# Three of seven butterflies of a spectral layer made by extra stage-3 matmuls instead of by VectorE

## The chip, the cores and the metric

The kernel runs on one core of one Trainium2 chip. The metric is device time in microseconds (us) of one execution; below it is the median of several runs. A profiled execution gives the trace. Its times count from the start of the recorded span, which is some 1.8 us shorter than the device time (181.9 us for 183.7).

The engines are TensorE (PE in the profile, its weight loads PEld), VectorE (DVE), ScalarE (ACT), GpSimd (POOL) and the DMA queues. In the traces read here TensorE, VectorE and ScalarE take up their instructions in program order; e5 below shows what that can cost, 0.67 us. The granted clock in some views is the share of TensorE's full clock that the profile shows.

## The reference

The layer is a layer norm, a two-dimensional real FFT over 2048 x 512, a multiplication with complex weights, the inverse FFT and a residual; then a second layer norm and a two-layer feed-forward part with a squared ReLU.

```python
x = A_x                                           # 1 x 2048 x 512, bf16
X = rfft2(layernorm(x)); X = X * (w_r + 1j*w_i)   # 2048 x 257 complex
h = x + irfft2(X)
u = relu(layernorm(h) @ w1 + b1)
out = h + (u * u) @ w2 + b2                       # inner size 1792
```

## The kernel before

The FFT along the sequence is split in two (stages 1 and 3 forward, 4 and 6 back), with the FFT along the row between them (2 and 5). The columns of stage 3 come in pairs: pr = 0 is special, and pairs 1 to 7 have a symmetry. For those, stage 3 makes only the sums A and B by four matmuls of 512 columns. ScalarE copies them from PSUM, where the matmuls leave their sums, to SBUF, the memory that VectorE reads here (AB), and VectorE forms the four results X as A plus or minus B: the butterfly, two operations of 128x512. Then VectorE multiplies X by the weights (mA, mB), combines them into Z, and forms M, the butterfly for the way back. Stage 4 on TensorE reads M.

```python
def stage2(pr):                       # cut
    U = fwd.tile([P, 2, 512], BF16, tag="U", bufs=3)
    # ... 8 matmuls of 256 columns into pu
    nc.scalar.copy(Uv, pu[:]...)

def stage3(pr):                       # pr > 0
    px = mm_tile("p3")
    nc.tensor.matmul(px[:, 0:512], lhsT=C, rhs=U[:, 0, :], start=True, stop=False)
    nc.tensor.matmul(px[:, 0:512], lhsT=Sn, rhs=U[:, 1, :], start=False, stop=True)
    nc.tensor.matmul(px[:, 512:1024], lhsT=C, rhs=U[:, 1, :], start=True, stop=False)
    nc.tensor.matmul(px[:, 512:1024], lhsT=Sp, rhs=U[:, 0, :], start=False, stop=True)
    nc.scalar.copy(AB[:]..., px[:])

def butterfly(pr):                    # cut: two VectorE operations, returned as a pair
    return (lambda: nc.vector.tensor_tensor(Xf[:, 0::3], AB[:, 0], bsw, ALU.add),
            lambda: nc.vector.tensor_tensor(Xf[:, 2:0:-1], AB[:, 0], bsw, ALU.subtract))

def spectral(pr):                     # one "round" of VectorE, cut
    nxt = butterfly(pr + 1) if pr + 1 < 8 else (lambda: None, lambda: None)
    # mA = X * w_r ; mB = X * w_i     two operations of 128x1024
    nxt[0]()
    # Z[:, :, 0] = mA - mB ; Z[:, :, 1] = mA + mB
    nxt[1]()
    # M[:, 0] = sum, M[:, 1] = difference of the halves of Z: two operations of 128x512

stage2(0); stage2(1); stage3(0); stage3(1); stage2(2)
# tables EI for pairs 1 to 3 (transposes on TensorE, copy on ScalarE)
stage3(2)
for pr in range(9):
    if 0 < pr and pr + 2 < 8:
        stage3(pr + 2)
    if pr + 3 < 8:
        stage2(pr + 3)
    if pr > 0:
        stage4(pr - 1)                # ScalarE copies its result to T2
    # pr >= 5: five matmuls that keep TensorE busy
    if pr < 8:
        spectral(pr)
    # pr == 0: EI of pairs 1, 3 negated on VectorE; tables EI for pairs 4 to 7 built
    # pr == 1: EI of pairs 4 to 7 negated on VectorE
    # pr == 4: table GI made by ScalarE (a sine)
```

"Round" below means one call of `spectral`, numbered by its pair. The order on ScalarE: it copies AB(k), then U(k+1), then the result T of stage 4.

## Time and profile before

| | before |
|---|---|
| device time, median of 3 runs | 183.8 us |
| TensorE, VectorE, ScalarE, GpSimd busy, share of the span | 88%, 67%, 56%, 26% |
| the spectral stage (26.4 to 52.1 us) | VectorE 3.22 us a round |
| the stretch after it (to 181.9 us) | 119.8 of 129.8 us busy on TensorE |

The view of busy time by stretch, for two rounds in the middle of the stage. After the two ends and the length come busy us (and number of instructions) of TensorE, its weight loads, VectorE, ScalarE and GpSimd, then the granted clock, the DMA share and GB/s:

```profile
36.30:39.50 3.20, 2.89 (x23) 2.05 (x22) 3.20 (x10) 2.96 (x4) 0.00 (x0) 1.00 0.00 0
39.50:42.80 3.30, 2.99 (x24) 2.15 (x22) 3.30 (x10) 3.06 (x5) 0.00 (x0) 1.00 0.02 5
```

VectorE is busy for the whole of both stretches.

### The profile page before, as it was taken

Reading aid. Unit: us, or ns where it says so; the run is one execution under the profiler, and the core shown is the slowest. Engines: PE = TensorE matmul, PEld = TensorE weight load, DVE = VectorE, ACT = ScalarE, POOL = GpSimd, SP = SyncE. Lnnn points to the kernel's source line nnn. Section 1 sums busy time; section 2 is a strip of 40 time slices with the busy share of each in tenths; the row PEclk is TensorE's granted clock in tenths of the full one; section 3 lists DMA queues with packets and bytes.
Section 4 is the critical chain, followed back from the end, with each engine's and each line's share of the span. In section 5 each row is a group of like instructions: output and inputs, shape, how many; then the busy total and the mean of one; then the engine's idle time right before and its main releaser. Section 6 shows DMA issues by size and latency. Waiting matters only on the chain.

```text
span 181.9 us, 2667 instructions
## 1 busy us (share of the span) xinstructions
PE 160.0 (88%) x946; PEld 89.0 (49%) x946; DVE 122.2 (67%) x297; ACT 101.8 (56%) x172; POOL 46.5 (26%) x83
## 2 busy tenths in 40 slices
PE   3676896989978787999999999999999989999991
PEld 1244564666534475456643545544544434556440
DVE  7986549999957277646897248697338795359311
ACT  4976879999634278037931367922357921268200
POOL 5889910000000250204402022422022422025000
PEclk9999999999999999999999999999999999999999
DMA  5999990000000000000000000001110000110010
GB/s 159 352 425 405 378 228 23 0 0 4 2 0 0 2 4 0 2 29 29 4 0 29 29 29 4 0 0 50 36 34 0 0 0 29 58 34 0 0 58 29
DMA packets 7773, 11.19 MB, mean 62 GB/s; under 512 B 2256, under 2 KB 6224, under 8 KB 7504
## 3 DMA queue, kind: packets, MB, share of 16 engines
q1 hardware_dynamic: 7600, 10.11, 16.3%
q0 software_dynamic: 160, 0.92, 1.2%
q8 instruction: 7, 0.11, 0.3%
q14 instruction: 6, 0.05, 0.1%
HBM read 8.93 MB, written 2.10 MB: 61 GB/s over the span
## 4 chain that ended last, share of the span: by engine, by line
PE 50%; DVE 29%; ACT 9%; POOL 6%; issue 4%; DVEq 0%; POOLq 0%; ACTq 0%
PE ph L570 22%; PE po L589 20%; DVE act L574 3%; PE p L473 3%; DVE mA L379 3%; DVE mB L379 3%; DVE hs L488 2%; ACT rl L573 2%; ACT Bt L241 2%; PE p L532 2%; DVE st L497 2%; DVE st L205 2%; DVE M L392 2%; DVE Z L384 2%; ACT junk L494 1%
## 5 line engine op out<-in xcount | busy, mean ns | idle before, releaser
L570 PE MATMUL ph<-UT,W 128*128 128x384 bf16 (+2 forms) x280 | 53.2, 336 | 0.7 <-ACT UT L536 0.5
L573 ACT ACTIVATE rl<-ph,b1f 128x384 bf16<-128x384 f32 (+2 forms) x70 | 41.2, 603 | 20.9 <-PE ph L570 19.5
L589 PE MATMUL po<-W,act 128*128 128x512 bf16 x224 | 50.8, 379 | 0.0
L574 DVE TENSOR_TENSOR act<-rl 128x384 bf16<-128x384 bf16 (+2 forms) x70 | 32.5, 477 | 17.2 <-ACT rl L573 16.9
L570 PEld LDWEIGHTS <-W 128*128 128x128 bf16 x280 | 27.4, 98 | 20.8 <-issue 1.4
L589 PEld LDWEIGHTS <-act 128*128 128x128 bf16 x224 | 21.6, 98 | 27.4 <-issue 3.1
L577 POOL TENSOR_TENSOR hb<-hs,b2b 128x512 f32<-128x512 bf16 x16 | 18.4, 1153 | 57.4 <-DVE act L574 55.4
L593 DVE TENSOR_TENSOR ot<-po,hb 128x512 bf16<-128x512 f32 x16 | 11.0, 689 | 18.1 <-PE po L589 18.1
L517 ACT ACTIVATE u<-hs,nm,rs 128x512 bf16<-128x512 bf16 x6 | 4.7, 808 | 25.2 <-DVE nm L514 25.2
L231 PE MATMUL p<-KFr,xs 128*128 128x256 bf16 x28 | 8.6, 334 | 4.7 <-DVE KFr L216 4.6
L488 DVE SCALAR_TENSOR_TENSOR hs<-p,xs 128x512 bf16<-128x512 f32 x16 | 10.8, 678 | 0.1
L473 PE MATMUL p<-GI,T 128*128 128x256 bf16 x64 | 9.4, 272 | 0.4 <-DVE T L415 0.4
L502 POOL TENSOR_TENSOR nm<-mv 128x1 f32<-128x1 f32 x5 | 1.5, 291 | 30.9 <-ACT junk L494 30.9
L246 PE MATMUL idle<-ones 128*128 128x512 bf16 x37 | 9.0, 379 | 0.0
L487 PE MATMUL p<-R,KI 128*128 128x512 bf16 x16 | 6.1, 381 | 3.2 <-DVE R L483 3.2
L233 PE MATMUL p<-KFr,xs 128*128 128x256 bf16 x28 | 8.6, 335 | 0.0
L246 PEld LDWEIGHTS <-ones 128*128 128x128 bf16 x45 | 4.7, 106 | 7.8 <-POOL ones L142 2.9
L205 DVE BATCH_NORM_STATS2 st<-xs 128x6 f32<-128x512 bf16 x13 | 8.3, 673 | 0.0
L360 ACT CAST AB<-p 128x1024 bf16<-128x1024 f32 x7 | 7.1, 1014 | 1.9 <-PE p L358 1.2
L417 ACT CAST T<-p 128x1024 bf16<-128x1024 f32 x7 | 7.2, 1025 | 1.8 <-PE p L410 1.8
L330 PE MATMUL p<-GF,Bt 128*128 128x256 bf16 x64 | 8.1, 273 | 0.0
L473 PEld LDWEIGHTS <-T 128*128 128x128 bf16 x64 | 6.2, 98 | 3.5 <-ACT T L414 0.9
(135 smaller groups left out, 220.5 us busy)
## 6 DMA issues: line engine op xcount, KB each, us to landing
W<-in_B_w_dram SPq DMA_DIRECT2D x2, 1792.0 KB, 19.7
out_dram<-ot SPq DMA_DIRECT2D x16, 128.0 KB, 1.8
xs<-in_A_x_dram SPq DMA_DIRECT2D x3, 512.0 KB, 5.9
WB<-in_A_w_r_dram SPq DMA_DIRECT2D x1, 1028.0 KB, 9.6
WB<-in_A_w_i_dram SPq DMA_DIRECT2D x1, 1028.0 KB, 12.2
xs<-in_A_x_dram SPq DMA_DIRECT2D x2, 256.0 KB, 3.4
b2b<-in_B_b_dram SPq DMA_DIRECT2D x1, 128.0 KB, 8.2
b1b<-in_B_b_dram SPq DMA_DIRECT2D x1, 3.5 KB, 22.8
```

What stands on the lines that cost most here:

```text
L205: nc.vector.bn_stats(st[:], xs[:, g, :])
L231: nc.tensor.matmul(o, lhsT=xs[:, g, P * t:P * t + P], rhs=KFr[:, g, 0:P].unsqueeze(1).to_broadcast([P, 2, P]), start=True, stop=False)
L246: nc.tensor.matmul(o, lhsT=ones[:, 0:P], rhs=ones[:], start=True, stop=True)
L379: nc.vector.tensor_tensor(m[:], X[:], w[:, pr:pr + step + 1:step, 1:Df].unsqueeze(2).to_broadcast([P, 2, 2, 256]), ALU.mult)
L473: nc.tensor.matmul(pe[:, 256 - 256 * e:512 - 256 * e], lhsT=T2[:, lt, g].rearrange("p q s -> p (q s)"), rhs=GI[:, lt, :], start=(r == 0), ...
L488: nc.vector.scalar_tensor_tensor(hs[:, g, :], py[:], WSC, xs[:, g, :], ALU.mult, ALU.add)
L570: nc.tensor.matmul(ph[:, 0:n], lhsT=W1[:, d, bass.ts(f, P)], rhs=UT[:, d, 0:n], start=(d == 0), stop=(d == ND - 1))
L573: nc.scalar.activation(rl[:, 0:n], ph[:, 0:n], ACT.Relu, bias=b1f[:, f:f + 1], scale=1.0)
L574: sq = nc.vector.tensor_tensor(act[:, f, 0:n], rl[:, 0:n], rl[:, 0:n], ALU.mult)
L577: add = nc.gpsimd.tensor_tensor(hb[:, g, :], hs[:, g, :], b2b[:], ALU.add)
L589: nc.tensor.matmul(po[:], lhsT=act[:, f, bass.ts(i, P)], rhs=W2[:, f, :], start=(f == 0), stop=(f == NF - 1))
L593: nc.vector.tensor_tensor(ot[:], po[:], hb[:, g, :], ALU.add)
```

## The change

VectorE is to be relieved. For pairs 2, 4 and 6, stage 3 makes all four results X itself: it accumulates the second half of the butterfly in PSUM with eight more matmuls of 256 columns. ScalarE then copies X instead of AB, and VectorE has no butterfly for these pairs. A negated cosine table Cn is added, and X gets a third buffer.

```diff
+    ON_PE = (2, 4, 6)
+    Cn = fwd.tile([P, len(ON_PE), P], BF16, name="Cn")
...
+    nc.vector.tensor_scalar(Cn[:], EF[:, ON_PE[0]:ON_PE[-1] + 1:ON_PE[1] - ON_PE[0], 1, :], -1.0, None, ALU.mult)
...
+        elif pr in ON_PE:
+            C, Sp, Sn, Cm = EF[:, pr, 1, :], EF[:, pr, 0, :], EF[:, pr, 2, :], Cn[:, ON_PE.index(pr), :]
+            px = mm_tile("p3")
+            for u in range(2):
+                o = px[:, 512 * u:512 * u + 512]
+                nc.tensor.matmul(o, lhsT=C, rhs=U[:, 0, :], start=True, stop=False)
+                nc.tensor.matmul(o, lhsT=Sn, rhs=U[:, 1, :], start=False, stop=False)
+                for r, (ws, wc) in enumerate(((Sp, C), (Sn, Cm)) if u == 0 else ((Sn, Cm), (Sp, C))):
+                    other = slice(256 - 256 * r, 512 - 256 * r)
+                    orr = o[:, 256 * r:256 * r + 256]
+                    nc.tensor.matmul(orr, lhsT=ws, rhs=U[:, 0, other], start=False, stop=False)
+                    nc.tensor.matmul(orr, lhsT=wc, rhs=U[:, 1, other], start=False, stop=(r == 1))
+            Xs[pr] = X = fwd.tile([P, 2, 2, 256], BF16, tag="X", bufs=3, name="X")
+            nc.scalar.copy(X[:].rearrange("p u r c -> p (u r c)"), px[:])
...
-        nxt = butterfly(pr + 1) if pr + 1 < 8 else (lambda: None, lambda: None)
+        nxt = butterfly(pr + 1) if pr + 1 < 8 and pr + 1 not in ON_PE else (lambda: None, lambda: None)
```

More of the change, by code (lines that the diff above doesn't have):

```diff
@@ L341, in stage3 @@
         if pr == 0:
-            Xs[pr] = X = fwd.tile([P, 2, 2, 256], BF16, tag="X", bufs=2, name="X")
+            Xs[pr] = X = fwd.tile([P, 2, 2, 256], BF16, tag="X", bufs=3, name="X")
             pxs = [mm_tile("p3"), mm_tile("p3b")]
@@ L351, in stage3 @@
                 cp(X[:, u].rearrange("p r c -> p (r c)"), pxs[u][:, 0:512])
+        elif pr in ON_PE:
[10 more added lines that the diff above has]
+                    nc.tensor.matmul(orr, lhsT=wc, rhs=U[:, 1, other], start=False, stop=(r == 1))
+            Xs[pr] = X = fwd.tile([P, 2, 2, 256], BF16, tag="X", bufs=3, name="X")
+            nc.scalar.copy(X[:].rearrange("p u r c -> p (u r c)"), px[:])
         else:
@@ L364, in butterfly @@
         AB = ABs[pr]
-        Xs[pr] = X = fwd.tile([P, 2, 2, 256], BF16, tag="X", bufs=2, name="X")
+        Xs[pr] = X = fwd.tile([P, 2, 2, 256], BF16, tag="X", bufs=3, name="X")
         bsw = AB[:, 1, ::-1, :]
```

## The prediction

> **What bounds the kernel now.** I read the shares of the final chain first, then that chain in order of time, then the timeline of one engine at a time between 22 and 66 us, where the changed code runs. The page says who carries the end:
>
> ```profile
> PE 50%; DVE 29%; ACT 9%; POOL 6%; issue 4%; DVEq 0%; POOLq 0%; ACTq 0%
> ```
>
> TensorE's half is the feed-forward part (from 62 us on), which the change does not touch. VectorE's share lies largely between 26 and 52 us, in the spectral stage. One of its eight rounds in the chain (columns: start us, us, what):
>
> ```profile
> 29.69 0.60 DVE mA L379
> 30.29 0.60 DVE mB L379
> 30.89 0.34 DVE X L369
> 31.23 0.33 DVE Z L384
> 31.56 0.34 DVE Z L385
> 31.90 0.33 DVE X L370
> 32.23 0.34 DVE M L392
> 32.57 0.33 DVE M L394
> ```
>
> The reader is to see eight operations without a hole: 2 x 0.60 + 6 x 0.335 = 3.22 us a round, and mA starts repeat at 36.25, 39.47, 42.69, 45.91 and 49.13 us: 3.22 apart. The two X lines are the butterfly of the next pair, 0.67 us. So the stage looks VectorE-bound. But a second loop runs at almost the same speed. TensorE (timeline, columns: start us, us, engine line operation, idle before):
>
> ```profile
> 37.66 0.38 PE L355 MATMUL p<-U,EF 128*128 128x512 bf16 x1 [0.31 <-ACT U L337]
> ...
> 38.30 0.38 PE L358 MATMUL p<-U,EF 128*128 128x512 bf16 x1
> ...
> 40.74 0.38 PE L355 MATMUL p<-U,EF 128*128 128x512 bf16 x1 [0.31 <-ACT U L337]
> ```
>
> and ScalarE:
>
> ```profile
> 38.76 1.01 ACT L360 CAST AB<-p 128x1024 bf16<-128x1024 f32 x1 [0.24 <-ACT T L417]
> 39.67 1.02 ACT L337 CAST U<-p 128x1024 bf16<-128x1024 f32 x1
> 40.58 1.03 ACT L417 CAST T<-p 128x1024 bf16<-128x1024 f32 x1
> ...
> 44.56 1.08 ACT L113 ACTIVATE GI<-fiI 128x1024 bf16<-128x1024 int16 x1
> 45.52 1.02 ACT L360 CAST AB<-p 128x1024 bf16<-128x1024 f32 x1
> ```
>
> Stage 3 of pair k runs from 37.66. Its result is copied (AB) from 38.76, 1.10 us later. ScalarE is in order, so the copy of the next U starts 0.91 us after that. Stage 3 of pair k+1 waits for that U and starts 1.07 us after it. 1.10 + 0.91 + 1.07 = 3.08 us: a closed loop of stage 3, its copy, the next U and the next stage 3. It has only 0.14 us a round less than VectorE. TensorE's idle 0.31 us lies inside the loop, waiting for ScalarE; it is no room for extra matmuls ahead of the AB copy.
>
> Last, VectorE's final round, which has no butterfly:
>
> ```profile
> 49.74 0.68 DVE L379 TENSOR_TENSOR mB<-X,WB 128x1024 bf16<-128x1024 bf16 x1
> 50.45 0.43 DVE L384 TENSOR_TENSOR Z<-mA,mB 128x512 bf16<-128x512 bf16 x1
> 50.79 0.42 DVE L385 TENSOR_TENSOR Z<-mA,mB 128x512 bf16<-128x512 bf16 x1
> 51.31 0.42 DVE L392 TENSOR_TENSOR M<-Z 128x512 bf16<-128x512 bf16 x1
> ```
>
> Without an X between them, mB to Z takes 0.71 us start to start instead of 0.60, and Z to M 0.52 instead of 0.34. The butterfly fills the time in which a result becomes visible.
>
> **What the Trainium skill says.** "TensorE: Matmul & The Clock Gate", section "Back-to-back issue gap", gives 262 cycles between isolated matmuls of 256 columns and 518 for 512, at 2.4 GHz 109 and 216 ns. The trace agrees: sixteen of 256 columns (L330) take 1.75 us, 109 ns each, and the four of stage 3 start 0.21 or 0.22 us apart. "Perfetto Trace Analysis", section "DVE / Act Engine Instruction", says the reported window runs on to the acknowledged write. The trace agrees: mB is listed with 0.68 us while an independent operation starts 0.60 us after it. I therefore count start to start. "VectorE: DVE Perf Modes", section "The DRAIN you can't avoid", says that a read after a write on the same engine needs a semaphore or an operation in between, and that in its test the semaphore cost nothing extra. The first fits the interleaving here; the second does not: 0.11 and 0.18 us are lost in the last round.
>
> **The change part by part.**
> Removed: the two X operations ahead of pairs 2, 4 and 6. On paper 3 x 0.67 = 2.01 us of VectorE, but each of those rounds (1, 3, 5) then looks like the last one and pays 0.11 + 0.18, so it saves 0.38 us, 1.1 us in all: rounds of 2.84 instead of 3.22.
> Added on VectorE: one negation Cn of 128x384. The EI negation of that size takes 0.28 us, 0.20 start to start. The order of instructions puts it behind the EF negation (20.66), where VectorE then idles 0.43 us until 21.64 us: hidden.
> Added on TensorE: stage 3 of pairs 2, 4, 6 has four matmuls of 512 and eight of 256 columns instead of four of 512: 8 x 0.109 = 0.87 us more each, 2.61 us in all. All of it comes before the copy, so it lies in the loop: 1.97 instead of 1.10 us.
> Moved: ScalarE's order is unchanged, with X copied in place of AB for these pairs (same 128x1024 shape, same 0.91). A third X buffer means that this copy waits for the multiply three pairs back, long done.
>
> Replay with these intervals, all in us (early rounds have 1.06 to 1.07 in place of 1.10, before the T copies begin). Stage 3 starts, before then after: pair 2 28.48, 28.48; pair 3 31.52, 32.40; pair 4 34.58, 35.47; pair 5 37.66, 39.40; pair 6 40.74, 42.47; pair 7 43.82, 46.40. Pair 7's copy comes in order behind U(7), T and the GI table: U(7) 45.33, T 46.24, GI 47.15, AB(7) 48.11 until 49.13 (before: 45.52 to 46.54). That is 3 x 0.87 = 2.61, less rounding, later.
> VectorE: round 1 starts at 29.61 as before and ends at 32.45, but the EI negation behind it now waits for the EI copy, which ScalarE starts behind U(3) at 32.25 and ends at 33.27. Round 2 starts at 33.5 (33.02 before), round 3 at 36.75, round 4 at 39.6. Its butterfly needs AB(5), whose copy ends 41.5, 0.7 after VectorE could use it; round 5 starts at 43.55, round 6 at 46.4. Its multiplies end at 47.6 and its butterfly waits for AB(7) until 49.15: 1.5 us idle. X, Z, Z, X, M, M take 2.0 us, so round 7 starts at 51.2 instead of 49.13: **2.05 us late**.
> Against the 2.61 us the difference is the slack there was: X(7) ran at 47.12 with AB(7) ready at 46.54.
> After round 7 all follows as before (stage 4, stage 5, then TensorE's stretch), so the 2.05 us goes through whole: 183.8 + 2.05 = 185.85.
>
> **The rivals.**
> First, VectorE stays the bound: then 1.1 us (0.4 a round) to 2.0 us are gained, 181.8 to 182.7. For it speaks the final chain, where VectorE is named without a break. Against it speaks that the other loop is only 0.14 us a round faster, so a mean of 0.44 us more per pair turns it over.
> Second, the added matmuls hide in TensorE's idle 0.3 us a round: then the loop grows by about 0.56 instead of 0.87 three times, and the time is near 184.9. Against it: that idle time is a wait for U, behind the copy that the added matmuls delay. It would need stage 3 to start earlier, which nothing in the change does.
> Third, the delay is worse: a longer last drain, an accumulation that stalls when matmuls alternate halves of a bank, or TensorE losing clock in its longer waits. Stage 3 of pair 0 already mixes 512 and 256 in one bank at 0.11 us a step, and the granted clock is 1.00 in all of this stage, so I give at most another 0.8 us.
>
> **Range and chances.** The centre is 185.8 us, 1.1% slower. Half a microsecond each way covers the waits I rounded and the 0.5 us of the EI negation; the first two rivals stretch the lower side a little: 184.8 to 186.6. Faster by over 2% would mean under 180.1, more than the removed operations hold: chance 0.01. Slower by over 2% means over 187.5, nearly twice the delay: 0.05. Within 2%: 0.94.
>
> **What would show it right or wrong.** In the profile after: stage 3 of pairs 2, 4 and 6 takes about 1.95 us to its copy; starts of stage 3 alternate near 3.95 and 3.08 us apart; VectorE waits on ScalarE's AB copy in the rounds before pairs 5 and 7, some 0.7 and 1.5 us, and on EI near 32.5 us for some 0.9 us; rounds 1, 3, 5 take 2.84 us, not 2.55; the last M starts near 53.7 instead of 51.65; and the stretch from there to the end has its old length. The chain before 52 us then names ScalarE and TensorE between the VectorE pieces. I am wrong if stage 3 of pair 3 starts before 32 us, or if VectorE has no waits in the stage. The later stretch changing length by itself would also break the sum.

## The result and the profile after

The kernel after takes 185.76 us (185.75 to 185.78, 4 runs) against 183.78 us before: the ratio is 1.0108, with a 95% interval from 1.009 to 1.0125. So it is 1.1% slower.

VectorE's busy time did fall, from 122.2 to 121.7 us of the whole, and TensorE's rose from 160.0 to 161.3. In the spectral stage alone VectorE's fell from 25.5 us (26.0 to 52.1) to 24.4 (26.0 to 54.1), 0.38 us for each of the three pairs. The shares of the final chain have moved:

```profile
PE 53%; ACT 17%; DVE 15%; POOL 6%; issue 3%; DMA 3%; SPq 0%; POOLq 0%; DVEq 0%; ACTq 0%
```

VectorE fell from 29% to 15% and ScalarE rose from 9% to 17%. The chain in order of time shows why (start us, us, what). Where it once listed one VectorE operation after another, it now reads:

```profile
37.45 0.84 ACT X L369
38.36 1.03 ACT U L340
39.43 0.38 PE p L373
...
40.49 0.89 ACT AB L378
41.42 1.02 ACT U L340
42.48 0.38 PE p L361
...
44.41 0.89 ACT X L369
```

This is the loop: copy of stage 3, copy of the next U, next stage 3. One turn with an ordinary pair (5) takes 42.48 - 39.43 = 3.05 us; the turn with pair 4 before it took 39.43 - 35.47 = 3.96 us. The timeline of TensorE shows the longer stage 3 of pair 6, its first and its last matmul:

```profile
42.48 0.38 PE L361 MATMUL p<-U,EF 128*128 128x512 bf16 x1 [0.28 <-ACT U L340]
...
44.10 0.27 PE L367 MATMUL p<-U,EF 128*128 128x256 bf16 x1
```

Its copy starts at 44.41, 1.93 us after 42.48, against 1.10 before. TensorE still idles 0.28 us ahead of the stage: the added matmuls did not use that gap. ScalarE, at the end of the loop:

```profile
47.16 1.07 ACT L115 ACTIVATE GI<-fiI 128x1024 bf16<-128x1024 int16 x1
48.12 1.01 ACT L378 CAST AB<-p 128x1024 bf16<-128x1024 f32 x1
```

AB(7) starts at 48.12 instead of 45.52. And VectorE, which had no hole between its rounds before, now waits (last column: idle time before the operation, and what ended it):

```profile
33.32 0.29 DVE L263 TENSOR_SCALAR EI<-EI 128x512 bf16<-128x512 bf16 x1 [0.92 <-ACT EI L260]
...
39.15 0.43 DVE L410 TENSOR_TENSOR M<-Z 128x512 bf16<-128x512 bf16 x1 [0.32 <-PE p L428]
...
41.53 0.43 DVE L387 TENSOR_TENSOR X<-AB 128x512 bf16<-128x512 bf16 x1 [0.41 <-ACT AB L378]
...
46.16 0.43 DVE L410 TENSOR_TENSOR M<-Z 128x512 bf16<-128x512 bf16 x1 [0.52 <-PE p L428]
...
49.16 0.43 DVE L387 TENSOR_TENSOR X<-AB 128x512 bf16<-128x512 bf16 x1 [1.03 <-ACT AB L378]
...
53.71 0.42 DVE L412 TENSOR_TENSOR M<-Z 128x512 bf16<-128x512 bf16 x1
```

In the kernel before, the last M was this:

```profile
51.65 0.42 DVE L394 TENSOR_TENSOR M<-Z 128x512 bf16<-128x512 bf16 x1
```

The last M starts at 53.71 instead of 51.65 us, 2.06 us later. From there to the end of the span it is 130.3 us in both (181.9 - 51.65, 184.0 - 53.71). So the spectral stage alone carries the difference.

### The profile page after: what moved, and what is told of

It is laid out like the page before. It is cut to its first block, busy times and chain, and to the rows that moved or that the text cites. A ratio compares the mean times of both kernels' runs of the same rounds, so it can differ in the third digit from the quotient of the medians. Undisturbed runs are those within 1.5% of the kernel's fastest.

```text
span 184.0 us, 2708 instructions
## 1 busy us (share of the span) xinstructions
PE 161.3 (88%) x970; PEld 90.8 (49%) x970; DVE 121.7 (66%) x292; ACT 101.7 (55%) x172; POOL 46.4 (25%) x83
## 4 chain that ended last, share of the span: by engine, by line
PE 53%; ACT 17%; DVE 15%; POOL 6%; issue 3%; DMA 3%; SPq 0%; POOLq 0%; DVEq 0%; ACTq 0%
PE ph L588 21%; PE po L607 20%; ACT U L340 4%; DVE act L592 3%; DMA xs<-in_A_x_dram 3%; PE p L491 3%; DVE hs L506 2%; ACT rl L591 2%; ACT AB L378 2%; ACT Bt L243 2%; PE p L550 2%; DVE st L515 2%; ACT junk L512 1%; POOL rs L523 1%; ACT X L369 1%
## 5 line engine op out<-in xcount | busy, mean ns | idle before, releaser
L592 DVE TENSOR_TENSOR act<-rl 128x384 bf16<-128x384 bf16 (+2 forms) x70 | 32.5, 478 | 17.2 <-ACT rl L591 16.9
L233 PE MATMUL p<-KFr,xs 128*128 128x256 bf16 x28 | 7.6, 305 | 5.8 <-DVE KFr L218 5.5
L554 ACT COPY UT<-p 128x768 bf16<-128x768 bf16 (+2 forms) x5 | 4.2, 842 | 6.5 <-PE p L550 6.5
L515 DVE BATCH_NORM_STATS2 st<-hs 128x6 f32<-128x512 bf16 x11 | 7.6, 689 | 0.2
```

The lines of the kernel that those rows point to most:

```text
L515: nc.vector.bn_stats(st[:], hs[:, g, :])
L592: sq = nc.vector.tensor_tensor(act[:, f, 0:n], rl[:, 0:n], rl[:, 0:n], ALU.mult)
```

## The experiments

The theory: a loop through TensorE and ScalarE (stage 3, its copy, the next U, the next stage 3) became the bound, because all added matmuls lie inside it. The main rivals: VectorE's saved work counts after all; or the added TensorE work is too much whatever the order. Ten kernels were run, all with five rounds (e1 has four runs, the others five). The kernel before, run beside them, took 183.72 us (e1 to e4), 183.71 (e5 to e8) and 183.68 (e9, e10); these three batches ran on three chips, so they agree to 0.04 us.

| run | what | us | ratio to before (95% interval) |
|---|---|---|---|
| e1 | before + the matmuls only | 185.77 | 1.0112 (1.0096 to 1.0127) |
| e2 | butterflies left out only (wrong result) | 183.12 | 0.9968 (0.9954 to 0.9982) |
| e3 | after, stage 2 ahead of stage 3 | 182.95 | 0.9959 (0.9945 to 0.9972) |
| e4 | before, stage 2 ahead of stage 3 | 183.90 | 1.0010 (0.9997 to 1.0024) |
| e5 | after, GI table late | 185.09 | 1.0074 (1.0060 to 1.0088) |
| e6 | e3, tables late, gaps filled with M | 182.39 | 0.9927 (0.9914 to 0.9941) |
| e7 | before, three X buffers | 183.79 | 1.0001 (0.9987 to 1.0015) |
| e8 | e3, tables late | 182.59 | 0.9939 (0.9925 to 0.9952) |
| e9 | e1, stage 2 ahead of stage 3 | 184.34 | 1.0035 (1.0021 to 1.0048) |
| e10 | e6, negations late, X ahead of Z | 182.24 | 0.9920 (0.9907 to 0.9934) |

### The two halves of the change, each alone

e1 adds to the kernel before as many matmuls, of the same size and at the same place, with a weight of zeros. The result stays correct and all butterflies stay on VectorE.

```diff
+    nc.gpsimd.memset(zw[:], 0.0)
...
     nc.tensor.matmul(px[:, 0:512], lhsT=Sn, rhs=U[:, 1, :], start=False, stop=not more)
+    if more:                          # pairs 2, 4, 6; the same after the second half
+        zeros(px[:, 0:512])           # four matmuls of 256 columns, lhsT=zw
```

> The kernel before with all seven butterflies on VectorE, and eight more matmuls of 256 columns with a weight of zeros in stage 3 of pairs 2, 4 and 6 (same result). Loop theory: 185.8 us like the full change, because VectorE's butterflies then run inside its waits for the pair 7 copy (ending near 49.15 us, last M start near 53.7). If the work removed from VectorE counted at all in the full change, this kernel would be slower than it by up to 1.1 to 2.0 us: 186.9 to 187.8. If the matmuls hid in TensorE's idle time: 183.8.

It took 185.77 us, as the full change did (185.76). VectorE of e1, at pair 7's butterfly and the last M:

```profile
49.26 0.43 DVE L384 TENSOR_TENSOR X<-AB 128x512 bf16<-128x512 bf16 x1 [0.37 <-ACT AB L375]
...
53.81 0.42 DVE L409 TENSOR_TENSOR M<-Z 128x512 bf16<-128x512 bf16 x1
```

With all seven butterflies VectorE still comes to pair 7 too early and waits. So in the full change the work taken from VectorE counts for nothing, and the added matmuls alone make the whole loss.

e2 is the other half: the kernel after with the four old matmuls for pairs 2, 4 and 6 and no butterfly. Its output is wrong, which doesn't matter for the time.

```diff
-            for u in range(2):
-                ...                   # twelve matmuls
+            nc.tensor.matmul(px[:, 0:512], lhsT=C, rhs=U[:, 0, :], start=True, stop=False)
+            ...                       # the four of the kernel before
```

> The kernel after without the added matmuls: the butterflies of pairs 2, 4, 6 are just left out, so the result is wrong on purpose. Loop theory: stage 3 starts stay 3.08 us apart, AB(7) ends at 46.5 us as before, VectorE comes to it about 0.6 us early and waits: 183.2 to 183.3 us, a gain of 0.5 us only. Rival, VectorE alone is the bound: 182.7 us if each butterfly is worth 0.38 us, 181.8 us if it is worth 0.67 us.

It took 183.12 us, 0.60 us less than before (its last M starts at 51.06 us against 51.65). Removing 2.0 us of VectorE operations gains only that, even when TensorE gets no more work; the loop theory had said 0.5. VectorE waits 0.41 us for AB(7), whose copy still starts at 45.46 us. Two things set that start. The loop, still at 3.05 to 3.08 us a turn, brings stage 3 of pair 7 to 43.75 us; and the GI table stands in front of the copy on ScalarE, so that it comes 1.71 us after that start and not 1.06, as in e5 below. By an estimate from these numbers, AB(7) without GI in front would be there by 45.85 us, before VectorE could use it at 46.01. So it is the loop and the GI table together, not the loop alone, that take the rest of the gain. No run has e2 with GI late.

### Opening the loop

e3 puts stage 2 of pair k+1 ahead of stage 3 of pair k. ScalarE then copies U(k+1) before the result of stage 3, and the next stage 3 no longer waits behind that copy. e4 does the same to the kernel before.

```diff
+    stage2(3)
     stage3(2)
     for pr in range(9):
+        if 0 < pr and pr + 3 < 8:
+            stage2(pr + 3)
         if 0 < pr and pr + 2 < 8:
             stage3(pr + 2)
-        if pr + 3 < 8:
-            stage2(pr + 3)
```

> The kernel after with stage 2 of pair k+1 put ahead of stage 3 of pair k, so that ScalarE copies U(k+1) before the result of stage 3 and the loop is open. Loop theory: TensorE no longer waits for U in the loop, added matmuls run in its spare time, AB(7) ends near 46.5 us and round 7 starts near 48.6 us: 183.2 us. Rival, TensorE's work itself is what bounds (added 2.61 us whatever the order): 185.8 us.

> Control: the kernel before with the same reorder. Loop theory: before the change VectorE's 3.22 us rounds bound, the loop had 0.14 us a round to spare, so opening it changes nothing: 183.8 us, at most 0.2 either way. If the loop had bound before as well: a gain of over 0.5 us.

e3 took 182.95 us: 2.8 us less than the kernel after, by order alone, with the same matmuls. AB(7) starts at 45.02 us instead of 48.12, and TensorE, which waited for U at each stage 3, has no wait listed between 28.5 and 48.3 us. The time is also 0.25 us less than expected: VectorE no longer waits for AB(7) at all. AB(7) in e3:

```profile
45.02 1.01 ACT L378 CAST AB<-p 128x1024 bf16<-128x1024 f32 x1
```

e4 took 183.90, no gain. So before the change the loop did not bind, and after it the loop did. The rival that TensorE's work itself bounds the kernel after is refuted.

e9 is e1 with this reorder, so that the matmuls alone are tried in an open loop.

> e1 (all butterflies on VectorE, added zero-weight matmuls) with the order of e3 and e4. It leaves the order as the only difference to e1. Loop theory: the same 2.61 us of matmuls now run beside VectorE: 183.9 us like e4, at most 184.2. If TensorE's work bounds whatever the order: 185.8 us like e1.

It took 184.34 us: 1.43 us less than e1, but 0.44 more than e4, where I had allowed 0.3. The trace shows where: VectorE waits 0.56 us for AB(2) in round 1 (e4 loses 0.19 there), while the pipeline is being filled and stage 3 of pair 2 is already the longer one. From round 2 on it goes at 3.22 us a round without a wait. So the matmuls are hidden once the loop is open, except for the first.

### The piece of ScalarE work inside the loop

e5 is the kernel after with the GI sine made in iteration 6 instead of 4 (a small GpSimd copy in the same branch moves with it).

```diff
-        if pr == 4:
+        if pr == 6:
             sin_of(GI[:].rearrange("p t c -> p (t c)"), fiI[:])
```

> The kernel after with the GI table (0.95 us on ScalarE, in order ahead of AB(7)) made two rounds later, where ScalarE idles. Loop theory: AB(7) then starts 1.08 us after stage 3 of pair 7, at 47.5 instead of 48.12 us, and VectorE's wait before X(7) shrinks from 1.03 to 0.4 us: 185.1 us, a gain of 0.6 us. If ScalarE's copy of pair 7 were not on the path: 185.8 us.

It took 185.09 us, 0.67 less than the kernel after; AB(7) moved from 48.12 to 47.47 and X(7) from 49.16 to 48.51, 0.65 us each. So the delay of AB(7) passes through to the end at its full size, as a path must.

### A version that beats both

e8 is e3 with the GI table late and the EI tables of pairs 4 to 7 built and negated one round later. e6 does in addition what the last-round listing in the prediction suggests: in rounds 1, 3 and 5, which have no butterfly to put between dependent operations, it puts the two M operations of the round before there.

```diff
+        if pr in (1, 3, 5):            # the M of pr-1 must come before stage4(pr-1)
+            spectral(pr)
         if pr > 0:
             stage4(pr - 1, split=(pr == 8))
...
-        nxt[0]()
+        first, second = late.pop(pr - 1, nxt)      # M of the round before, or the butterfly
+        first()
         nc.vector.tensor_tensor(Z[:, :, 0], ...)
         nc.vector.tensor_tensor(Z[:, :, 1], ...)
-        nxt[1]()
+        second()
```

> e3 with the two table moves of e6 but without the M operations put into the gaps: it tells the two parts of e6 apart. Expected 182.6 us: 0.33 us less than e3 from the wait for AB(3) that goes, nothing from the GI move since VectorE no longer waits for AB(7).

> Best version I can form: e3 with the GI table late, the EI tables of pairs 4 to 7 one round later, and in rounds 1, 3 and 5, which have no butterfly, the two M operations of the round before put between multiply and Z and between Z and M. If each unfilled round loses 0.29 us (0.11 + 0.18) as the trace says, three of them give 0.87 us and the AB(3) wait another 0.33 us: 181.7 to 181.9 us, the last M start near 49.8 us. If TensorE, busy without a hole from 28.5 us in e3, is the next bound: 182.3 to 182.6 us.

e8 took 182.59 us as expected. e6 took 182.39: it missed its 181.8 and lies in the range given for TensorE as the next bound. Filling three rounds gained 0.20 us, not 0.87. Round 3 of e6 does run eight operations in 3.22 us without a hole (mA at 35.33, next mA at 38.55), so the filling itself works. But VectorE now waits at other places in its timeline:

```profile
29.15 0.29 DVE L263 TENSOR_SCALAR EI<-EI 128x384 bf16<-128x384 bf16 x1 [0.19 <-ACT EI L260]
...
35.12 0.29 DVE L263 TENSOR_SCALAR EI<-EI 128x512 bf16<-128x512 bf16 x1 [0.18 <-ACT EI L260]
```

Besides these, X(5) starts 0.72 us after the start of mB instead of 0.60, when AB(5)'s copy ends, and the multiply behind the second X(5) operation follows 0.45 us after it instead of 0.335. Together that is 0.6 us. These waits do not say what the bound is, though. X(5) starts at 39.88 us in e6, and in e8, which fills no round, at nearly the same time:

```profile
39.91 0.43 DVE L387 TENSOR_TENSOR X<-AB 128x512 bf16<-128x512 bf16 x1
```

So what the filling of rounds 1 and 3 gained went into waits ahead of X(5). From X(5) to the start of the last M it is 10.45 us in e6 and 10.64 in e8, and this is the whole gain of 0.2 us.

e10 tries to take the waits of e6 away: the negations one round later still, and the second X ahead of the second Z, so that X is not the operation just before its multiply.

> e6 with the two EI negations one round later and the second X ahead of the second Z in rounds 0, 2, 4. e6 missed its 181.8 by 0.55 us; its trace shows VectorE waiting 0.19 and 0.18 us at the negations, 0.12 us for AB(5) and losing 0.12 us between X(5) and the multiply after it. If AB(5), which comes from a TensorE that is busy without a hole, fixes the time of X(5), only the last 0.12 us is gained: 182.2 to 182.3 us. If the waits simply add up: 181.8 us.

It took 182.24 us, at the value for "TensorE fixes X(5)". The two waits at the negations are gone and have moved to AB(5):

```profile
39.94 0.43 DVE L387 TENSOR_TENSOR X<-AB 128x512 bf16<-128x512 bf16 x1 [0.53 <-ACT AB L378]
```

X(5) is at 39.94 us in e10, at 39.88 in e6 and at 39.91 in e8, whatever VectorE does before it. The final chain of e10 shows what leads there:

```profile
36.14 1.01 ACT X L369
37.16 0.75 ACT T L443
37.95 1.03 ACT U L340
38.99 0.93 ACT AB L378
39.94 0.43 DVE X L387
```

Before 36.14 us it lists TensorE's matmuls without a hole of over 0.05 us, back to the filling of the pipeline; from there four ScalarE copies follow each other some 0.9 us apart, X(4), T, U and AB(5). So TensorE fixes X(4), and ScalarE's order of copies carries that on to AB(5). Stage 3 of pair 5 starts at 37.69 us, so that by its usual 1.06 to 1.10 us AB(5) could have started only some 0.1 us before its 38.86 (an estimate). e10 is 0.8% faster than the kernel before and is the best version found. That these two engines fix X(5) is read from the traces: no run with fewer matmuls on pairs 2 and 4, or with fewer copies in between, was made to show it.

### The third X buffer

e7 is the kernel before with X in three buffers.

```diff
-        Xs[pr] = X = fwd.tile([P, 2, 2, 256], BF16, tag="X", bufs=2, name="X")
+        Xs[pr] = X = fwd.tile([P, 2, 2, 256], BF16, tag="X", bufs=3, name="X")
```

> Control: the kernel before with three X buffers instead of two and nothing else. VectorE idles 0.50 us before the first multiply in every run with two X buffers and not in those with three; the next operation then waits for AB(1) for 0.2 us. So 183.6 to 183.7 us, at most 0.1 us gained. If the third buffer carried part of the gain of e3: 183.3 us or less.

It took 183.79 us, no difference, and my reading of the early gap was wrong: VectorE still idles 0.50 us before the first multiply (26.57 us), with three buffers as with two. The gap stands in the traces of before, e1, e4, e7 and e9, and is missing in all kernels in which X of some pair is made by ScalarE. What causes it stays open. It is worth at most 0.1 us, since the operation after the multiplies waits for AB(1) where the gap is missing (0.21 us in the kernel after).

## Why the prediction was right

- **Time.** 185.8 predicted, 185.76 measured.
- **The loop of 3.08 us becomes the bound.** Shown. Starts of stage 3 were predicted at 32.40, 35.47, 39.40, 42.47 and 46.40 us for pairs 3 to 7; they are at 32.42, 35.47, 39.43, 42.48 and 46.41. e3 shows that order, and not the amount of work, makes the loss.
- **Added matmuls.** 1.97 us from the start of stage 3 to its copy was predicted; 1.93 to 1.98 was measured. The hidden negation Cn is as foreseen: it runs at 21.08 us, and the operation that follows the gap is at 21.67 in place of 21.64.
- **The GI table in front of AB(7).** 48.11 predicted, 48.12 measured; e5 shows that it lies on the path, and that 0.67 of the 1.98 us lost go with its place.
- **The wait for EI.** Some 0.9 us near 32.5 was predicted; it is 0.92 us, ending at 33.32.
- **The saving of 0.38 us for a butterfly, not 0.67.** Round 1 has mB to Z 0.72 us apart in place of 0.60. In e3, where nothing else interferes, rounds 3 and 5 take 2.87 us, so 0.35 us is saved for each.
- **One step was incomplete.** Rounds 3 and 5 of the kernel after were to take 2.84 us and took 3.08 and 3.29. M waits for stage 4 of two pairs back, which reads the same one of two M buffers and is now late itself (the two waits named PE p L428 above). I had not followed that buffer. It changed nothing, since VectorE then waits for AB(5) and AB(7) anyway: those waits, predicted as 0.7 and 1.5 us, shrank by those 0.24 and 0.45 us, to 0.49 and 1.11 counted from start to start.
- **One reading was loose, and one stays open.** VectorE's share of the final chain is not "largely" between 26 and 52 us: the pieces listed there add up to some 24.5 us, under half of the 29% (some 53 us). It does not enter the sum. And that the semaphore test in the Trainium skill does not fit the trace is not shown (see the end).
- **The rivals.** "VectorE stays the bound" and "the matmuls hide in TensorE's idle time" are refuted by the result itself and by e1; no extra loss of the third kind appeared. A gain was there to be had once the copy order was changed: e3.

## What to carry to other kernels

An engine that is busy all the time in a stage is not the only bound there: look for a closed loop through other in-order engines and compare its time per turn with the busy engine's. Here it was 3.08 against 3.22 us, so little could be won by relieving the busy engine alone (e2: 0.60 us for 2.0 us of operations removed), and work moved into the loop delayed its end, AB(7), by its full 2.60 us, of which the slack there hid only some 0.6. Idle time of an engine inside such a loop is a wait, and it becomes room only when the order of the copies is changed so that the loop opens.

## What the Trainium skill lacked or had wrong

- "Perfetto Trace Analysis", section "Identifying the Most-Contended Engine", says to optimise the engine with the highest occupancy first. VectorE was busy 3.20 of 3.20 us here; the change took 2.0 us of operations from it and lost 1.98 us, and e1 shows that the removed work was worth nothing there. No page that I read tells how to find a dependence loop across in-order engines that runs almost as slowly as the busiest engine.
- "VectorE: DVE Perf Modes", section "The DRAIN you can't avoid", reports that eight copies on VectorE took as long with a semaphore after each as with one after the last, so that the semaphore cost nothing extra. It gives no cost for waiting on a result. Here an operation that reads the result of the one just before it starts 0.11 us later (mB to Z) or 0.18 us later (Z to M) than an independent one. Whether the two contradict is open: the page does not say that its copies read each other's results, and no run here takes a semaphore out. In its favour: one operation in between does remove the loss, as that section says it removes the hazard (e6, round 3).
- "TensorE: Matmul & The Clock Gate", section "Back-to-back issue gap", gives a sustained 131 ns for matmuls of 512 columns in a stream with weight loads, and 81 ns for 128 columns. Streams with weight loads here run at 216 ns for 512 columns (42 matmuls in 9.08 us in the chain of the kernel before) and some 55 ns for 128 columns (stage 4 of pair 0). Those are the page's isolated figures; the sustained ones did not appear.
